# A two-dimensional transform and two feed-forward layers on one core: the lone rows' share computed once and added to the sums of a group

## The chip, the cores and the metric

The kernel runs on one core of a Trainium2 chip. A core has a matrix engine (TensorE; PE for its products, PEld for its weight loads), VectorE (DVE), ScalarE (ACT), GpSimd (POOL) and SyncE (SP), which here only issues DMAs; 16 DMA engines move data between HBM and the on-chip memory SBUF. Products are summed in PSUM. The metric is the time of one execution on the device, in microseconds, as the median of several runs.

## The reference

```python
def _attn_ref(x):                      # x: 8 x 3072 x 256
    X = np.fft.fft(x, axis=1)
    X = np.fft.fft(X, axis=2)
    return X.real.astype(np.float32)

def _moe_ref(x, w_in, w_out):          # w_in 256 x 2048, w_out 2048 x 256
    h = x @ w_in
    g = h - np.tanh(h)
    return (g @ w_out).astype(np.float32)

def _moe2_ref(x, w_in, w_out, g_ln):   # w_in 256 x 1024, w_out 1024 x 256
    h = x @ w_in
    e = np.exp(h - np.max(h, axis=-1, keepdims=True))
    sm = e / (np.sum(e, axis=-1, keepdims=True) + 1e-09)
    solu = h * sm
    mu = np.mean(solu, axis=-1, keepdims=True)
    var = np.mean((solu - mu) ** 2, axis=-1, keepdims=True)
    ln = (solu - mu) / np.sqrt(var + 1e-06) * g_ln
    return (ln @ w_out).astype(np.float32)
```

The transform's 8 x 3072 rows are the tokens of the first layer, whose output is the input of the second.

## The kernel before

The program has two parts that follow each other.

**The transform.** The 3072 rows of a batch are taken in sets of eight that the transform along the sequence treats alike; there are 384 such places, in three blocks (j = 0, 1, 2) of 128. With 8 batches that makes 24 iterations q = 3b + j. For each, SP loads a block `x` of 1 MB (`load_next("x")`, L296, three buffers). DVE adds and subtracts its parts (`prep`: `sm` L440, `cv` L445, `pm` L450, for j = 1 also L456), and PE multiplies the result with tables of cosines and sines (`transform`: `odd_class` L479, `even_classes` L498 and L507; tables `tts`, loaded by `table`, L352). The sums of a batch fill the eight PSUM banks, and after j = 2 `evict` copies them with ACT to `zt` and on to DRAM (`z1_d`, `z2_d`).

The first of the 384 places stands for no full set: its rows, 0, 384, 768 and so on of each batch, are the *lone rows*, eight per batch. They are loaded as `x8` (three copies of eight rows in partitions 0, 32 and 64, for a high and a low half). DVE and ACT turn them into `hl8` (`prep_8`: L416, L166, L169). For every batch PE adds their share to the sums, with four products against the small table `t8s`, whose columns repeat with a period of four (`lone_products`, L518).

The same loop prepares the weights. Twelve pieces are loaded in the order of `w_when`, narrowed from 64-bit words by two ACT steps (L201, L202) and three DVE steps (`narrow`: L205, L208, L211), and stored or, for the first four, multiplied with a table (`fold_w_in`, L389). `weave` interleaves such works with the preparation of iteration q + 2 step by step; the order of instructions on each engine is the program's order. The Nyquist column is loaded as `nraw` (L651) and `n8`, and prepared by `prep_nu` (L575 to L581), which is woven with `prep(3)`; `transform_nu` (L611) comes ahead of `transform(3)`.

**The loop.** 48 groups of 256 column pairs (six per batch), 16 steps each. In each step PE computes a block of the first layer (`ab`, L847), DVE adds the rank-one part and forms two halves (L858, L870, L871), ACT takes tanh (L877), DVE subtracts (L882), ACT rounds to a high half `gh` (L166), and POOL makes the low half (L169). `o1` (L901) multiplies high and low halves two steps later; its six products per step are in the order high, high, low. `layer2` spreads the second layer of the group before over the steps (products L934, L1039 and L1046; store by POOL at L1088 at every fourth step).

For the next group, `load_z` loads even and odd sums `zf` from DRAM at step 3. At step 7 `sum_z` adds and subtracts them for both halves u (L271, four POOL instructions of 128 columns), and at step 11 the results `zc` are split into high and low `zs`. For the first two groups this work is done on DVE, in the transform (iterations 15 and 18).

Issues of DMAs: SP's queue takes nearly all; ACT's takes the stores of `z2_d`. Eight semaphores count the landings of the DMAs of both.

Of the kernel before, what the change touches and what calls it, by code (L numbers as in the profile page):

```python
# [82 lines left out]
def tables():  # L83
# [18 lines left out]
    t24 = np.concatenate([c2, -c2, c4, s2, s4, -s4], 1)  # L102
# [6 lines left out]
    t8 = np.stack([np.cos(ang(k, r, 8)), np.sin(ang(k, r, 8)) * sign], 1).reshape(8, 2, 3, 4)  # L109
    t8h, t8l = split(t8)  # L110
    t8x = np.zeros((96, 2, 3, 4), np.float32)
# [28 lines left out]
def fft2_moe_moe_kernel(  # L140
# [11 lines left out]
    wo_d = dram.tile([4, P, 4, D], F32, name="wo_d")  # L152
    wi2_d = dram.tile([2, P, FF2], F32, name="wi2_d")
# [8 lines left out]
    z1536 = keep.tile([P, 3, B], F32, name="z1536")  # L162
    zh = keep.tile([P, 2, B], F32R, name="zh")
# [74 lines left out]
    t8s = tab.tile([96, 2, 3, 4], F32R, name="t8s")  # L238
    hl8 = tab.tile([96, B, 256], F32R, name="hl8")
# [89 lines left out]
    for q, w in zip((8, 11, 14, 16, 18, 20, 22, 23), w_rest):  # L329
# [18 lines left out]
    def table(j, k):  # L348

        edges = (0, 2 * NS, 2 * NS + TU, TT)  # L350
        o = slice(edges[k], edges[k + 1])
        nc.sync.dma_start(out=tts[:, j, o], in_=tt[j * P : (j + 1) * P, o])  # L352
# [4 lines left out]
    for i in range(8):  # L357
        pn = ps.tile([P, 512], F32, tag="ps", name=f"p_none{i}")
        for _ in range(3 if i < 6 else 2):
# [3 lines left out]
    for parts in ([(0, 0)], [(0, 1), (0, 2)], [(1, 0)]):  # L363
# [45 lines left out]
    def prep_8():  # L409
        r8 = raws.pop("x8").rearrange("p (b d) -> p b d", b=B)[0:96]  # L410
        parts = []
        for i in range(2):
            bs = slice(i * B // 2, (i + 1) * B // 2)
            eo8 = scratch(f"eo8_{i}").rearrange("p (b d) -> p b d", b=B // 2)[0:96]
            for u, op in ((0, ALU.add), (1, ALU.subtract)):
                nc.vector.tensor_tensor(  # L416
                    out=eo8[:, :, u * P : (u + 1) * P], in0=r8[:, bs, :P], in1=r8[:, bs, P:], op=op
                )
            rnd(hl8[:, bs], eo8)
            parts.append((bs, eo8))  # L420
            yield
# [870 lines left out]
```

## Time and profile before

| | |
|---|---|
| median of three runs | 2693.86 us (2693.49 to 2694.44) |
| the profiled execution: its time, its span | 2695.17 us, 2693.4 us |
| PE products, weight loads, busy | 2679.4 us, 2396.0 us |
| DVE, ACT, POOL busy | 2361.1 us, 1874.9 us, 2105.7 us |
| first product of the loop | 159.66 us after the span's start |
| mean granted PE clock | 0.999 of 2.4 GHz |

The span runs from the first to the last instruction that the profiler recorded. Busy time counts the instructions of an engine while they execute, not its waits and not the issue of DMAs. An average over the span hides that the transform and the loop have different limits, so times below are those of stretches.

### The profile page before, as it was taken

The page shows a single profiled execution, that of the slowest core. Times are in us where ns is not written, and L with a number is a line of the kernel's source. Part 1 is how long each engine was busy: PE and PEld are TensorE (multiplying, and loading weights), DVE is VectorE, ACT ScalarE, POOL GpSimd, SP SyncE. Part 2 cuts the span into 40 slices and gives each one's busy share as a digit, 9 for nine tenths or more (in the row PEclk, how much of TensorE's full clock was granted, in tenths as well). Part 3 has the DMA queues.
Part 4 walks back from the last instruction along what each step waited for, and adds up shares of the span by engine and source line. Part 5 has one row for each costly group of instructions (what it writes and reads, how often), then busy time and mean ns, then how long its engine had stood idle before and what let it go on. Part 6 is the DMA issues. An engine that isn't in the chain of part 4 may idle for free.

```text
span 2693.4 us, 47817 instructions
## 1 busy us (share of the span) xinstructions
PE 2679.4 (99%) x15348; PEld 2396.0 (89%) x15348; DVE 2361.1 (88%) x4789; ACT 1874.9 (70%) x3414; POOL 2105.7 (78%) x2786
## 2 busy tenths in 40 slices
PE   9999999999999999999999999999999999999999
PEld 5688999999999999999999999999999999999998
DVE  8988898888988888888988888888888889888886
ACT  3566777777777777777777777777777777767776
POOL 0057888888888888888888888888888888888885
PEclk9999999999999999999999999999999999999999
DMA  9953444444444444444444444444444444444442
GB/s 367 364 195 70 98 95 100 102 95 95 108 96 95 101 102 96 94 106 98 95 106 97 98 95 107 95 95 108 95 99 99 102 95 96 106 97 99 97 95 52
DMA packets 882842, 303.29 MB, mean 113 GB/s; under 512 B 788528, under 2 KB 844080, under 8 KB 879296
## 3 DMA queue, kind: packets, MB, share of 16 engines
q1 hardware_dynamic: 879984, 293.74, 44.0%
q10 hardware_dynamic: 2304, 6.42, 0.6%
q8 instruction: 123, 2.02, 0.3%
q14 instruction: 127, 1.04, 0.1%
q0 software_dynamic: 304, 0.07, 0.0%
HBM read 161.55 MB, written 138.60 MB: 111 GB/s over the span
## 4 chain that ended last, share of the span: by engine, by line
PE 92%; DVE 5%; DMA 1%; issue 1%; ACT 1%; POOL 0%; ACTq 0%; SPq 0%; DVEq 0%
PE x2p L901 36%; PE ab L847 19%; PE ph L934 18%; PE po L1039 12%; PE po L1046 6%; DVE cv L445 1%; DVE sm L440 1%; DVE pm L450 1%; DMA tts<-tt 0%; DMA wi_d<-wi_f 0%; DMA wo<-w_out 0%; DVE g L882 0%; DVE wi_f L211 0%; PE pt L1020 0%; POOL gh L169 0%
## 5 line engine op out<-in xcount | busy, mean ns | idle before, releaser
L901 PE MATMUL x2p<-gh,wo 128*128 128x512 f32 x4608 | 1122.5, 380 | 1.4 <-POOL gh L169 1.2
L169 POOL TENSOR_TENSOR gh<-g,gh 128x512 fp32r<-128x512 f32 x768 | 986.9, 1285 | 173.1 <-ACT gh L166 173.0
L901 PEld LDWEIGHTS x2p<-gh,wo 128*128 128x128 f32 x4608 | 826.6, 190 | 105.3 <-POOL gh L169 3.1
L877 ACT ACTIVATE t<-h 128x512 f32<-128x512 f32 x758 | 453.7, 599 | 462.7 <-DVE h L871 380.1
L847 PEld LDWEIGHTS ab<-zs,wt 128*128 128x128 f32 x4608 | 633.8, 191 | 43.6 <-ACT zt L566 2.3
L847 PE MATMUL ab<-zs,wt 128*128 128x256 f32 x4608 | 638.6, 275 | 1.9 <-ACT zt L566 1.6
L882 DVE TENSOR_TENSOR g<-h,t 128x512 f32<-128x512 f32 x758 | 514.4, 679 | 142.1 <-ACT t L877 120.6
L166 ACT ACTIVATE gh<-g 128x512 fp32r<-128x512 f32 x768 | 480.8, 626 | 153.4 <-DVE g L882 152.1
L934 PE MATMUL ph<-wi,x2s 128*128 128x512 f32 x2304 | 561.6, 380 | 1.1 <-POOL x2s L169 1.1
L169 POOL TENSOR_TENSOR ut<-um,ut 128x512 fp32r<-128x512 f32 x372 | 478.1, 1285 | 56.2 <-ACT ut L166 56.2
L1039 PE MATMUL po<-wo,ut 128*128 128x512 f32 x1528 | 521.4, 382 | 0.0
L934 PEld LDWEIGHTS ph<-wi,x2s 128*128 128x128 f32 x2304 | 421.7, 190 | 53.3 <-POOL x2s L169 1.5
L858 DVE SCALAR_TENSOR_TENSOR asb<-nb,wnu,ab 128x256 f32<-128x256 f32 x768 | 362.7, 472 | 85.4 <-PE ab L847 63.1
L1046 PE MATMUL po<-wo,ut 128*128 128x256 f32 x1528 | 416.5, 273 | 0.0
L870 DVE TENSOR_TENSOR h<-asb,ab 128x256 f32<-128x256 f32 x758 | 324.9, 429 | 26.1
L871 DVE TENSOR_TENSOR h<-asb,ab 128x256 f32<-128x256 f32 x758 | 324.6, 428 | 26.2
L1039 PEld LDWEIGHTS po<-wo,ut 128*128 128x128 f32 x1528 | 289.9, 190 | 30.3
L1046 PEld LDWEIGHTS po<-wo,ut 128*128 128x128 f32 x1528 | 293.4, 192 | 0.0
L949 ACT ACTIVATE e<-ph,st 128x1024 f32<-128x1024 f32 x192 | 214.9, 1119 | 96.7 <-PE x2p L901 60.3
L944 DVE TENSOR_REDUCE st<-ph 128x1 f32<-128x1024 f32 x192 | 233.6, 1217 | 4.5 <-PE ph L934 4.4
L958 DVE SCALAR_TENSOR_TENSOR u<-ph,e 128x1024 f32<-128x1024 f32 x192 | 233.6, 1217 | 3.5 <-ACT e L949 1.6
L166 ACT ACTIVATE ut<-um 128x512 fp32r<-128x512 f32 x372 | 233.5, 628 | 0.0
(123 smaller groups left out, 2229.7 us busy)
## 6 DMA issues: line engine op xcount, KB each, us to landing
mv_d<-tb SPq DMA_DIRECT2D x186, 512.0 KB, 2.6
um<-mv_d SPq DMA_DIRECT2D x744, 128.0 KB, 3.8
out<-o SPq DMA_DIRECT2D x192, 128.0 KB, 1.7
x<-xr SPq DMA_DIRECT2D x23, 1024.0 KB, 10.3
zf<-z_d SPq DMA_DIRECT2D x64, 128.0 KB, 2.7
z_d<-zt ACTq DMA_DIRECT2D x16, 392.0 KB, 7.3
wi<-w_in SPq DMA_DIRECT2D x6, 1024.0 KB, 9.2
z_d<-zt SPq DMA_DIRECT2D x16, 384.0 KB, 10.2
```

Of the source, the lines that this page charges most:

```text
L166: nc.scalar.activation(out=o, in_=i, func=AF.Copy)
L169: eng.tensor_tensor(out=o, in0=i, in1=hi.bitcast(F32), op=ALU.subtract)
L847: nc.tensor.matmul(in_pairs(pab[:, u]), wt[c][:, hw, u, o : o + P], in_turn(zs[:, hz, u]), start=(i == 0), stop=(i == 2),)
L858: nc.vector.scalar_tensor_tensor(out=asb, in0=zg[n][1], scalar=wnu[:, m : m + 1], in1=pab[:, 0], op0=ALU.mult, op1=ALU.add)
L870: nc.vector.tensor_tensor(out=h[:, 0], in0=asb, in1=pab[:, 1], op=ALU.add)
L871: nc.vector.tensor_tensor(out=h[:, 1], in0=asb, in1=pab[:, 1], op=ALU.subtract)
L877: nc.scalar.activation(out=t, in_=h, func=AF.Tanh)
L882: nc.vector.tensor_tensor(out=g, in0=hs.pop((n, m)).rearrange("p u n -> p (u n)"), in1=ts_.pop((n, m)).rearrange("p u n -> p (u n)"), op=A ...
L901: nc.tensor.matmul(in_pairs(x2p[n][mt]), wo1[c][:, hw, k, mt * P : (mt + 1) * P], in_turn(gh[:, hg]), start=(m == 0 and i == 0), stop=(m = ...
L934: nc.tensor.matmul(in_pairs(ph[:, fs]), xs[:, hx, k], in_turn(wi2[:, hw, k, fs]), start=(k == 0 and q == 0), stop=(k == 1 and q == 2),)
L1039: nc.tensor.matmul(in_pairs(po), ut[:, 0, ks], wo2[:, k].rearrange("p h x n -> p (x n) h"), start=(k == 0), stop=False,)
L1046: nc.tensor.matmul(in_pairs(po[:, :D]), ut[:, 1, ks], wo2[:, k, :, 0].rearrange("p h n -> p n h"), start=False, stop=(k == NK2 - 1),)
```

## The change

The lone rows' share of the transform has only 20 distinct columns for each batch and half u: four for each class, and four columns of two kinds again with the sign or the turn that the second window of a group needs. After the change PE computes these columns once (`lone_rows`, 16 products of 20 columns in iteration 3), ACT copies them to the tile `lone`, and `sum_z` adds them, repeated, to the sums of a group (`add_lone`): on POOL in the loop, on DVE for the first two groups. The four products per batch go. `lone` also goes into the special column `z1536`.

```diff
+    lone = keep.tile([P, B, 2, 5, 4], F32, name="lone")
...
+    def add_lone(n, u, eng, o):
+
+        b, g = divmod(n, GPB)
+        h, rows = g - NSJ, lone[:, b, u]
+        if h <= 0:
+            o = o.rearrange("p (a c) -> p a c", c=4)
+            add = rows[:, 1 if h == 0 else 0].unsqueeze(1).to_broadcast([P, GP // 4, 4])
+        else:
+            s = 4 if h == 1 else 2
+            o = o.rearrange("p (s a c) -> p s a c", s=s, c=4)
+            add = rows[:, 1:5] if h == 1 else rows[:, 2:5:2]
+            add = add.unsqueeze(2).to_broadcast([P, s, GP // 4 // s, 4])
+        return eng.tensor_tensor(out=o, in0=o, in1=add, op=ALU.add)
+
     def sum_z(n, u, eng):
...
+        return add_lone(n, u, eng, o)
...
-    def lone_products(u, lone, stop=False):
-        for pss, i, n in ((acc[1, u], slice(0, 1), NS), (acc[2, u], slice(1, 3), 2 * NB)):
...
+    def lone_rows():
+        pl = ps.tile([P, 512], F32, tag="ps", name="pl")[:, : B * 40].rearrange("p (b u k) -> p b u k", b=B, u=2)
+        for b in range(B):
+            for u in range(2):
+                nc.tensor.matmul(
+                    pl[:, b, u],
+                    hl8[u][:, b * P : (b + 1) * P].bitcast(F32R),
+                    t8s[:, u].rearrange("p c k -> p (c k)"),
+                    start=True,
+                    stop=True,
+                )
+        nc.scalar.copy(out=lone.rearrange("p b u c k -> p b u (c k)"), in_=pl)
...
         if q == 3:
             transform_nu()
+            lone_rows()
...
             for u in range(2):
-                if j == 7:
+                if j == 6 + u:
                     sum_z(n + 1, u, nc.gpsimd)
```

The beginning is rearranged. The lone rows are loaded once, as 64 rows, on ACT's queue; DVE and ACT split them, ACT stores the halves to DRAM and loads them back, in six DMAs, into the three places of two tiles that POOL has set to zero.

```diff
+    hl8 = [fold.tile([P, 1024], F32, tag="cw", bufs=4, name=f"hl8_{u}")[:96] for u in range(2)]
+    for h in hl8:
+        nc.gpsimd.memset(h, 0.0)
+    r8 = zp.tile([P, GP], F32, tag="nb", name="r8")[: 8 * B]
+    s8 = zp.tile([P, 2, 2, GP], F32R, tag="zs", name="s8")[: 8 * B, 0]
+    nc.scalar.dma_start(out=r8, in_=x8[0:8].rearrange("r b d -> (r b) d"))
...
     def prep_8():
...
+        eo8 = zp.tile([P, GP], F32, tag="zc", name="eo8")[: 8 * B]
+        for u, op in ((0, ALU.add), (1, ALU.subtract)):
+            nc.vector.tensor_tensor(out=eo8[:, u * P : (u + 1) * P], in0=r8[:, :P], in1=r8[:, P:], op=op)
+        rnd(s8[:, 0], eo8)
+        rest(nc.vector, s8[:, 1], eo8, s8[:, 0])
+        nc.scalar.dma_start(out=s8_d, in_=s8.bitcast(F32))
+        rows = s8_d.rearrange("(r b) w (u d) -> r w u b d", b=B, u=2)
+        for g, w in enumerate((0, 0, 1)):
+            for u in range(2):
+                to = hl8[u][32 * g : 32 * g + 8].rearrange("p (b d) -> p b d", b=B)
+                nc.scalar.dma_start(out=to, in_=rows[:, w, u])
```

The tables of the even classes come without their negatives (two thirds of the columns); ACT computes these for j = 0 and 2. The loads of tables and of x stand in another order, the products of zeros at the start are 27 in place of 22, in three banks in place of eight, and the last six pieces of the weights are loaded and narrowed one iteration earlier.

```diff
-    t24 = np.concatenate([c2, -c2, c4, s2, s4, -s4], 1)
+    t24 = np.concatenate([c2, c4, s2, s4], 1)
...
-    for q, w in zip((8, 11, 14, 16, 18, 20, 22, 23), w_rest):
+    for q, w in zip((8, 11, 13, 15, 17, 19, 21, 22), w_rest):
...
-        if q == 3 - 1:
-
-            coming["x"].append(("x8", lambda raw: [(raw[0:96], x8.rearrange("p b d -> p (b d)"))]))
...
+    def negatives(j):
+        for u, (at, of) in enumerate(((1, 0), (2, 1))):
+            nc.scalar.activation(out=triple(j, u)[:, at], in_=triple(j, u)[:, of], func=AF.Copy, scale=-1.0)
...
-    for parts in ([(0, 0)], [(0, 1), (0, 2)], [(1, 0)]):
+    for parts in ([(0, 0)], [(0, 1), (0, 2), (1, 0)], [(1, 1), (1, 2)]):
         load_next("x")
...
     now, folds = [], []
+    prep_8()
     weave(prep(0))
-    for j, k in ((1, 1), (1, 2), (2, 0), (2, 1), (2, 2)):
+    negatives(0)
+    for j, k in ((2, 0), (2, 1), (2, 2)):
         table(j, k)
...
     weave(prep(2))
+    negatives(2)
     load_next("w")
-    weave(prep_8())
     weave(prep(3), prep_nu())
```

## Rows read from the trace of the kernel before

**Rows 1.** The page, part 1: busy time, share of the span and instructions.
```profile
PE 2679.4 (99%) x15348; PEld 2396.0 (89%) x15348; DVE 2361.1 (88%) x4789; ACT 1874.9 (70%) x3414; POOL 2105.7 (78%) x2786
```

**Rows 2.** Windows: stretch, length, busy us of each engine, clock, DMA, GB/s.
```profile
10.00:20.00 10.00, 7.59 (x24) 3.98 (x22) 9.21 (x14) 0.00 (x0) 0.00 (x0) 1.00 1.03 346
...
100.00:125.00 25.00, 25.00 (x112) 17.11 (x112) 25.00 (x36) 12.99 (x22) 1.70 (x3) 1.00 1.01 366
...
1000.00:1052.00 52.00, 52.00 (x304) 47.33 (x303) 46.62 (x102) 37.40 (x69) 43.97 (x59) 1.00 0.43 100
```

**Rows 3.** Timeline, end of the transform: start, us, engine, line, operation, idle before.
```profile
150.14 1.29 DVE L450 TENSOR_TENSOR pm<-cv 128x512 f32<-128x512 f32 x2
...
151.55 0.96 PE L518 MATMUL pz<-t8s,hl 96*128 96x384 f32 x4
...
152.44 2.95 PE L479 MATMUL pz<-tts,pm 64*128 64x384 f32 x16
...
155.12 2.90 PE L498 MATMUL pz<-tts,pm 64*128 64x392 f32 x16
...
157.10 1.60 ACT L556 COPY zt<-pz 128x384 f32<-128x384 f32 x4
...
159.66 1.60 PE L847 MATMUL ab<-zs,wt 128*128 128x256 f32 x12 [1.63 <-ACT zt L566]
```

**Rows 4.** Timeline, beginning.
```profile
11.90 2.80 PE L498 MATMUL pz<-tts,pm 128*128 128x392 f32 x8
...
16.12 0.38 SPq L651 DMA_DIRECT2D nraw<-xn  x1
...
19.07 2.49 DVE L416 TENSOR_TENSOR eo<-x 96x512 f32<-96x512 f32 x4
...
25.75 1.23 DVE L440 TENSOR_TENSOR sm<-x 128x1024 f32<-128x1024 f32 x1 [1.81 <-DMA x<-xr]
...
26.90 0.18 DVE L575 TENSOR_TENSOR nraw<-nraw 128x32 f32<-128x32 f32 x1
```

**Rows 5.** Groups by line and shape, PE: busy us, mean ns | idle.
```profile
L822 PE MATMUL aside<-zh,wt 128*128 128x8 f32 x48 | 5.8, 245 | 0.0
```

**Rows 6.** Groups by line and shape, DVE.
```profile
L169 DVE TENSOR_TENSOR hl<-eo,hl 32x1024 fp32r<-32x1024 f32 x2 | 2.4, 1212 | 0.0
...
L169 DVE TENSOR_TENSOR zs<-zc,zs 128x256 fp32r<-128x256 f32 x4 | 1.5, 416 | 0.0
...
L205 DVE TENSOR_SCALAR wo_f<-wo_f 128x1024 f32<-128x1024 f32 x6 | 4.1, 688 | 1.6 <-ACT wo_f L201 1.6
...
L208 DVE SCALAR_TENSOR_TENSOR wo_f<-wo_f,wo 128x1024 uint32<-128x1024 uint32 x6 | 7.3, 1221 | 0.4 <-ACT wo L202 0.4
```

**Rows 7.** DMA issues up to 160 us: KB, median us to landing.
```profile
nraw<-xn SPq DMA_DIRECT2D x1, 96.0 KB, 9.9
```

**Rows 8.** Waits of SP's queue: us in total, times, longest.
```profile
SPq L296 <- DMA x<-xr: 13.3, 7, 3.0
```

**Rows 9.** The page, part 6: a short transfer on a nearly idle queue.
```profile
out<-o SPq DMA_DIRECT2D x192, 128.0 KB, 1.7
```

**Rows 10.** Groups by line and shape, POOL.
```profile
L1088 POOL TENSOR_TENSOR o<-o 128x256 f32<-128x256 f32 x191 | 140.9, 738 | 13.7 <-ACT o L1056 13.7
```

**Rows 11.** Timeline of the loop, POOL and PE, steps 6 to 9 of a group.
```profile
1002.52 1.29 POOL L169 TENSOR_TENSOR gh<-g,gh 128x512 fp32r<-128x512 f32 x1 [0.62 <-ACT gh L166]
...
1004.18 1.46 PE L901 MATMUL x2p<-gh,wo 128*128 128x512 f32 x6
...
1004.38 0.74 POOL L169 TENSOR_TENSOR x2s<-x2f,x2s 128x256 fp32r<-128x256 f32 x1 [0.57 <-PE ab L847]
...
1005.07 1.52 POOL L271 TENSOR_TENSOR zc<-zf 128x128 f32<-128x128 f32 x4
...
1010.65 1.29 POOL L169 TENSOR_TENSOR gh<-g,gh 128x512 fp32r<-128x512 f32 x1
...
1012.01 1.46 PE L901 MATMUL x2p<-gh,wo 128*128 128x512 f32 x6
```

More of the change, by code (lines that the diff above doesn't have):

```diff
@@ L237, in fft2_moe_moe_kernel @@
     tts = tab.tile([P, NSJ, TT], F32, name="tts")
[L238 to L239 removed]
+    t8s = tab.tile([96, 2, 5, 4], F32R, name="t8s")
+    hl8 = [fold.tile([P, 1024], F32, tag="cw", bufs=4, name=f"hl8_{u}")[:96] for u in range(2)]
[4 more added lines that the diff above has]
+    nc.scalar.dma_start(out=r8, in_=x8[0:8].rearrange("r b d -> (r b) d"))
     wnu = keep.tile([P, NM], F32, name="wnu")
@@ L348, in table, with triple @@
     def table(j, k):
-        edges = (0, 2 * NS, 2 * NS + TU, TT)
-        o = slice(edges[k], edges[k + 1])
-        nc.sync.dma_start(out=tts[:, j, o], in_=tt[j * P : (j + 1) * P, o])
+        if k == 0:
+            nc.sync.dma_start(out=tts[:, j, : 2 * NS], in_=tt[j * P : (j + 1) * P, : 2 * NS])
+            return
+        src = tt[j * P : (j + 1) * P, 2 * NS + (k - 1) * 2 * NB : 2 * NS + k * 2 * NB]
+        to = triple(j, k - 1)[:, 0 : 4 - k : 3 - k]
+        nc.sync.dma_start(out=to, in_=src.rearrange("p (t n) -> p t n", t=2))
+    def triple(j, u):
+        return tts[:, j, 2 * NS + u * TU : 2 * NS + (u + 1) * TU].rearrange("p (t n) -> p t n", t=3)
+    def negatives(j):
+        for u, (at, of) in enumerate(((1, 0), (2, 1))):
+            nc.scalar.activation(out=triple(j, u)[:, at], in_=triple(j, u)[:, of], func=AF.Copy, scale=-1.0)
     nothing = wt[3][:, 0, 0]
     nc.vector.memset(nothing.bitcast(F32), 0.0)
-    for i in range(8):
+    for i in range(3):
         pn = ps.tile([P, 512], F32, tag="ps", name=f"p_none{i}")
-        for _ in range(3 if i < 6 else 2):
+        for _ in range(9):
             nc.tensor.matmul(pn, nothing[:, :P], nothing, start=True, stop=True)
-    for parts in ([(0, 0)], [(0, 1), (0, 2)], [(1, 0)]):
+    for parts in ([(0, 0)], [(0, 1), (0, 2), (1, 0)], [(1, 1), (1, 2)]):
         load_next("x")
@@ L409, in prep_8 @@
     def prep_8():
[L410 to L421, printed above, removed]
-        load_next("x")
-        for bs, eo8 in parts:
-            yield rest(nc.vector, hl8[64:96, bs], eo8[64:96], hl8[64:96, bs])
+        eo8 = zp.tile([P, GP], F32, tag="zc", name="eo8")[: 8 * B]
[9 more added lines that the diff above has]
+                nc.scalar.dma_start(out=to, in_=rows[:, w, u])
     FOLDED = 1
@@ L483, in odd_class, with even_classes @@
                     start=(half == 0 and j == w),
-                    stop=(j == 2 and half == 1 and not (last_lone and w == 0)),
+                    stop=(j == 2 and half == 1),
                 )
-    def even_classes(q, u, pss, last_lone):
+    def even_classes(q, u, pss):
         j = q % NSJ
@@ L502, in even_classes @@
                         start=(half == 0 and j == w),
-                        stop=(j == 2 and half == 1 and not (last_lone and w == 0)),
+                        stop=(j == 2 and half == 1),
                     )
@@ L534, in transform @@
         b, j = divmod(q, NSJ)
-        def lone():
-            for u in range(2):
-                lone_products(u, hl8[:, b, u * P : (u + 1) * P], stop=(b == 0))
-        if j == 2 and b:
-            lone()
         for cls, products in ((1, odd_class), (2, even_classes)):
@@ L545, in transform @@
                     acc[cls, u] = sums(f"pz{b}_{cls}_{u}")
-                products(q, u, acc[cls, u], b == 0)
-        if j == 2 and not b:
-            lone()
+                products(q, u, acc[cls, u])
         hl.pop(q)
@@ L563, in evict @@
                 if b == B - 1:
-                    nc.gpsimd.tensor_tensor(out=z1536[:, 2], in0=z1536[:, 0], in1=z1536[:, 1], op=ALU.subtract)
+                    z = z1536[:, 2]
+                    nc.gpsimd.tensor_tensor(out=z, in0=z1536[:, 0], in1=z1536[:, 1], op=ALU.subtract)
+                    nc.gpsimd.tensor_tensor(out=z, in0=z, in1=lone[:, :, 0, 2, 0], op=ALU.add)
             for w, p in enumerate(acc.pop((2, u))):
```

14 lines of the change are left out of this document (4 added, 10 removed).

## The prediction

> **What bounds the kernel now.** I read the page first. The matrix engine (PE) is busy 99% of the span, VectorE (DVE) 88%, GpSimd (POOL) 78% [rows 1]: a change can matter only where it shortens what PE waits for, or makes it wait. The span has two parts, and I asked for the windows of each. In the loop (1000 to 1052 us, one group of 16 steps) PE is busy for all of the 52 us, POOL for 43.97, DVE for 46.62: PE sets the pace there, and nothing of this change takes PE work out of the loop. In the transform, which lasts until the loop's first product at 159.66, PE *and* DVE are full at once: both 25.00 of 25.00 us from 100 to 125 [rows 2].
>
> Which of the two sets the transform's end decides this case, and the timeline of its end answers it. DVE prepares the rows of iteration q two iterations ahead of PE. It finishes the last preparation (pm, q = 23) at 150.14 + 1.29 = 151.43; PE starts that iteration at 152.44, after the lone products of 151.55 [rows 3]. So at the end PE is only 1.0 us behind DVE. DVE itself has, from 26.90 on, nothing to wait for; the window from 100 to 125 shows it without a hole [rows 2]. Its work from 26.90 to 151.43 is a rigid block of 124.5 us, and whoever shortens PE by more than 1.0 us finds DVE as the bound. The block begins at 26.90 with nraw (the Nyquist column), behind x3, whose sums ran from 25.75 after 1.81 us of waiting for a DMA [rows 4].
>
> **The change part by part.**
>
> *Lone products out of PE.* Four matmuls per batch, from 151.55 to the next instruction at 152.44, 0.9 us [rows 3]: 8 x 0.9 = 7.2 us of PE go. In come 16 matmuls of 20 columns, each with 128 weight columns. Nearest row: the 48 matmuls of 8 columns at L822, 5.8 us, 0.12 each [rows 5]: +1.9 us once, in iteration 3. Net -5.3 us for PE; but only 1.0 us of it can be seen unless DVE's block moves too.
>
> *Lone rows out of DVE's beginning.* Four sums of 96x512, 2.49 us from 19.07 [rows 4], and two lows of 32x1024, 2.4 us [rows 6], become two 64x128 sums and one 64x256 low ahead of the first preparation. A 128x256 step takes 0.42 [rows 6], so the new ones cost under 1.3 us, and what hides them is that DVE later waits for nraw in any case; without that wait they would shift the block by that much. For the same reason the 4.9 us that go do not come off the start of the block: it starts when nraw has landed. The load of nraw stays behind the load that prep(1) issues. That was x3 and becomes x4, because x8 no longer takes a place in the queue. Bytes ahead of nraw: less 0.79 MB (x8) and 0.60 MB (a third of six tables), plus 1.05 MB (x4), plus 0.39 MB on ACT's queue (r8, s8 out to DRAM, six loads of 32 KB). At the 346 GB/s of the window from 10 to 20 [rows 2] the first three make -1.0 us, the ACT transfers +1.1. (The Trainium skill, "DMA: Bandwidth & Descriptors", section "Issuing engines are not separate DMA queues", has DMAs of all issuing engines interleave on the same 16 DMA engines. By that rule the +1.1 stands; a queue of its own would make it 0.) nraw was issued at 16.12 and took 9.9 us [rows 4, 7]: it landed at 26.0 and lands near 26.1. DVE would take it at once, 0.8 earlier than 26.90.
>
> Against that stands a limit on the DMAs under way. Seven issues at the line that loads x waited 13.3 us in all for another load of x to land, up to 3.0 at a time [rows 8]; by the order of issues that other one is the eighth before. r8 and the seven DMAs of prep_8 now stand in this row ahead of x3, so x3 may be issued only when a table (1,1) or (1,2) is in and SP's queue has run dry. I price the hole at up to 1.7 us, what a short transfer on an idle queue takes from issue to landing [rows 9]. So the block starts between 1.9 us earlier (ACT's bytes cost nothing, no hole) and 0.9 later. I take 0.0, the hole being nearly certain and its size not.
>
> *Added to DVE's block.* The first two groups' sums get four adds of 128x256 on DVE: 0.416 each [rows 6], less the overlap of some 0.04 that such rows show in a chain: +1.5 us (bounds: 1.1, and 3.0 if the repeated operand doubled them). The weights of iteration 22 move to 21, the one that prep(23) is woven into: two of their three DVE steps, 0.688 and 1.221 [rows 6], less 0.08 overlap each, now come before the last pm: +1.75. They ran after it so far.
>
> *End of the transform.* PE's last product ends at 155.12 + 2.90 = 158.02. ACT began to empty the sums at 157.10, because it narrowed the last weights first, and the loop's first product waited until 159.66 for it [rows 3]. With the weights one iteration earlier four copies of 0.4 run beside the last products; what remains after them is the copies of the even sums. I take 0.4 us off, bounds 0 and 0.8.
>
> *Negatives, copies.* Four ACT steps of 128x196 and one copy of 128x320, each under the 0.4 of a copy of 384 columns [rows 3]. ACT does nothing from 10 to 20 us [rows 2], which hides the first two if ACT isn't held by its own DMA issues (a rival below).
>
> *The loop.* 46 groups get two adds of 128x256 on POOL. Nearest row: 0.738, contiguous [rows 10]; the sums of 128 columns beside them read two runs of 64 and take 1.52 for four [rows 11], no more per column. I take 0.74 for each. They lie in POOL's gaps. Sums and add of u = 0 now come at step 6, ahead of the gh of 1002.52: 0.76 + 0.74 = 1.50 into a gap of 0.62, so that gh ends 0.88 later, at 1004.69. PE needs it for the fifth of the six matmuls from 1004.18, which start (1.46 - 0.38)/5 = 0.216 apart: at 1005.04, 0.35 to spare. The gap of 0.57 before x2s leaves 0.31 of lateness; step 7 does 1.50 in place of 1.52. The gh from 1010.65 ends at 1011.94 and is needed at 1012.01 + 0.86: 0.93 to spare against 0.3 [rows 11]. Cost: nothing; at most 2 us where groups have less slack.
>
> *Sum.* Last pm: 151.43 + 0.0 + 1.5 + 1.75 = 154.7. PE starts q = 23 there in place of 152.44: +2.25. Less 0.4 at the end: +1.85 us; loop 0. The profiled execution took 2695.17 us with a span of 2693.4; the median of the runs is 2693.86, 1.3 lower, and the shift goes onto the median: **2695.7 us**. The ends of the terms make -0.9 (-1.9, 1.1, 0.8 off) and +6.6 (+0.9, 3.0, no gain at the end, 2 in the loop; the 1.75 in both, the 1.0 of PE's lag off); ends do not come together, and 2693 to 2699 holds nearly all of this case.
>
> **The rivals.**
>
> *DVE gives way and PE's gain is seen (faster).* If PE stayed the bound, the end would move by -5.3 and -0.4: 2688.2 us. For it: DVE does lose 4.9 us of work, and x3 comes early. Against it: the last pm would have to be done at about 147, so the block, 3.25 longer, would have to start at 19, before x4 and nraw can be in. Chance 0.10, part gains included.
>
> *POOL's adds are dear (slower).* At a price c for an add the lateness is 0.76 + c - 0.62 - 0.57 after x2s and 2c - 1.19 after step 7; PE stalls once that passes 0.93, so from c = 1.06 us. At twice the contiguous row, 1.48, the stall is 0.84 us in each of 46 groups: +39 us, 2734. For it: no row has an operand repeated in runs of four columns. Against it: runs of 64 cost nothing extra [rows 11]. Chance 0.10. The Trainium skill, "GPSIMD Engine Reference", section 7, speaks for this rival: many small read commands cost about 102 cycles each, without overlap. By that rule, were each of the 64 repeats a command of its own, one add would take some 5 us (an estimate from that page); no row here shows such an operand.
>
> *The beginning holds PE up (slower).* ACT issues the loads of hl8 itself, each behind s8's way to DRAM and one of the eight, and the negatives stand behind them in ACT's order. PE's even products of q = 0, at 11.90 so far [rows 4], wait for the negatives, perhaps until 18. That alone is hidden: PE would be ready for q = 23 at 152.44 - 7 x 0.9 + 1.9 + 6.1 = 154.1, just before DVE's 154.7. If the granted clock fell to its lower level in that hole and some 8 us of products took twice as long, PE would be 7 us behind DVE: 2703 us. Against it: the clock is 1.00 from 10 to 20 us, where PE is busy only 7.59 of 10 [rows 2]. Chance 0.06.
>
> **How the numbers follow.** DVE as the bound, no difference that counts: 0.74. The rivals: 0.10, 0.10, 0.06. A difference of 0.2%, 5.4 us, is about what a measurement of this kernel can tell from none. The likeliest case lies inside it but for 0.02 on the slow side: faster 0.10, same 0.72, slower 0.18. The range reaches from 2691 (part gains of the first rival) to 2701 (lesser forms of the two others).
>
> **What would show it.** Right: no lone products in L518's place; DVE without a hole from about 27 to 155; PE with small waits on pm in the last iterations, where it had none; the loop's first product between 160 and 163; POOL's new adds near 0.74, and PE still 52.0 of 52 us per group. Wrong: that first product before 158 or after 165; an add over 1.06 us; x2p products that wait for gh; a granted clock under 1 before 40 us.

## The result, and the profile after

The changed kernel takes 2712.59 us (median of 6 runs, 2710.39 to 2714.84), the kernel before on the same chip 2694.51: a ratio of 1.0066, 95% interval 1.0053 to 1.0079. It is slower by 18 us. Predicted were 2695.7 us and a range of 2691 to 2701. The profiled execution took 2713.05 us with a span of 2711.2, against 2693.4 before.

Windows first, the stretches of [rows 2] and of the loop's start, of the changed kernel:

```profile
10.00:20.00 10.00, 3.53 (x11) 1.82 (x10) 8.58 (x14) 0.36 (x2) 0.00 (x0) 0.99 0.63 234
20.00:32.00 12.00, 11.40 (x45) 7.90 (x47) 3.36 (x5) 0.99 (x4) 0.00 (x0) 0.87 1.03 378
42.00:50.00 8.00, 8.00 (x26) 4.84 (x26) 7.86 (x12) 1.42 (x4) 0.00 (x0) 0.79 1.03 427
100.00:125.00 25.00, 18.57 (x68) 11.28 (x67) 20.08 (x29) 10.39 (x19) 1.43 (x2) 0.87 0.85 299
172.00:225.00 53.00, 50.68 (x296) 45.38 (x295) 42.38 (x88) 34.50 (x63) 37.07 (x30) 0.97 0.29 99
225.00:278.00 53.00, 49.45 (x276) 43.84 (x275) 42.51 (x88) 34.03 (x62) 39.50 (x51) 0.94 0.30 69
1000.00:1052.00 52.00, 52.00 (x305) 47.33 (x304) 47.17 (x107) 37.10 (x69) 44.68 (x61) 1.00 0.43 98
```

The loop's group is untouched: PE still 52.00 of 52, POOL 44.68 in place of 43.97. All 17.8 us of span are lost ahead of 278 us, in three places: the beginning (the DMAs move 234 GB/s from 10 to 20, before 346), the middle (DVE 20.08 of 25 from 100 to 125, before 25.00) and the loop's first groups.

The end of the transform divides them; timeline of it, changed kernel:

```profile
163.48 1.28 DVE L478 TENSOR_TENSOR pm<-cv 128x512 f32<-128x512 f32 x2
...
165.60 2.96 PE L507 MATMUL pz<-tts,pm 64*128 64x384 f32 x16
...
171.12 1.16 PE L874 MATMUL ab<-zs,wt 128*128 128x256 f32 x8
```

The loop's first product moved from 159.66 [rows 3] to 171.12, by 11.5 us; the other 6.3 are lost between there and 278 us. DVE's last pm is done at 164.76 (before 151.43), and the lone products are gone from the place ahead of 165.60.

**The beginning.** Timeline, changed kernel:

```profile
12.76 6.83 ACTq L452 DMA_DIRECT2D hl<-s_d  x6
...
18.63 0.89 SPq L376 DMA_DIRECT2D tts<-tt  x2
19.64 0.62 ACT L383 ACTIVATE tts<-tts 128x196 f32<-128x196 f32 x2 [15.71 <-DMA hl<-s_d]
19.65 0.34 SPq L320 DMA_DIRECT2D x<-xr  x1
...
20.06 3.76 PE L526 MATMUL pz<-tts,pm 128*128 128x392 f32 x6 [4.71 <-ACT tts L383]
...
32.08 0.19 DVE L599 TENSOR_TENSOR nraw<-nraw 128x32 f32<-128x32 f32 x1 [3.70 <-DMA nraw<-xn]
```

and the waits of SP's queue up to 32 us:

```profile
SPq L376 <- DMA hl<-s_d: 7.8, 1, 7.8
```

Read the two queues side by side. ACT issues the six loads of hl8 (L452) from 12.76 to 19.59, because they wait for s8 to be in DRAM and for turns among the transfers under way; the negatives (L383) come behind them, at 19.64. SP's next two table loads wait 7.8 us for the first of those same loads, so x3 is issued at 19.65 and nraw at 23.35 (before 16.12 [rows 4]). nraw is in at 32.08: DVE's block starts 5.2 us later. PE's even products of q = 0, at 11.90 before [rows 4], run at 20.06, six of them in 3.76 us where eight took 2.80: the lower of the clock's two levels, 1.2 GHz, behind a wait of 4.71.

**The middle.** Timeline, changed kernel:

```profile
118.29 1.13 ACT L205 ACTIVATE wo_f<-wo 128x1024 f32<-128x1024 f32 x1 [9.14 <-DMA wo<-w_out]
120.35 1.60 ACT L578 COPY zt<-pz 128x384 f32<-128x384 f32 x4
...
120.86 4.63 PE L420 MATMUL pw<-wi_f,ftab 128*128 128x512 f32 x5 [6.12 <-ACT zt L578]
```

ACT has come to narrow w_out before it is loaded. It waits 9.14 us; behind it in ACT's order stand the copies that empty the sums, behind those PE, and DVE has only 20.08 us of work in 25. The load itself was issued late, 5.6 us before ACT got it, because SP first waited 9.3 us for DVE's last narrowing step of an earlier piece, whose buffer the load takes:

```profile
SPq L320 <- DVE wi_f L215: 9.3, 1, 9.3
...
112.66 0.38 SPq L320 DMA_DIRECT2D wo<-w_out  x1
```

**The loop's start.** Timeline, ACT's second gh and then a stretch of step 6 of the loop's second group, changed kernel:

```profile
181.06 0.63 ACT L170 ACTIVATE gh<-g 128x512 fp32r<-128x512 f32 x1 [3.70 <-DMA z_d<-zt]
...
232.64 0.78 POOL L280 TENSOR_TENSOR zc<-zf 128x128 f32<-128x128 f32 x2
233.50 0.61 POOL L294 TENSOR_TENSOR zc<-zc,lone 128x256 f32<-128x256 f32 x1
234.06 1.27 POOL L173 TENSOR_TENSOR gh<-g,gh 128x512 fp32r<-128x512 f32 x1
...
235.38 1.22 PE L928 MATMUL x2p<-gh,wo 128*128 128x512 f32 x2 [2.38 <-DVE asb L885]
```

and the same place of the kernel before:

```profile
217.67 1.27 POOL L169 TENSOR_TENSOR gh<-g,gh 128x512 fp32r<-128x512 f32 x1
...
219.00 0.75 PE L901 MATMUL x2p<-gh,wo 128*128 128x512 f32 x2 [0.96 <-POOL gh L169]
```

The first line is a wait for storage: the tile gh may be written only when the store of zt has left the place where gh now lies. In the others, POOL's sums and add for u = 0 (1.4 us) have slipped in ahead of gh, in a group in which POOL also splits w_out2. That gh ends at 235.33, and PE, which starts at 235.38, has waited 2.38 us in place of 0.96 (the row names DVE's `asb`, which ended at 235.37; in the kernel before PE went on ahead of that step). The two windows from 172 to 278 us of the kernel before:

```profile
172.00:225.00 53.00, 51.64 (x289) 45.46 (x289) 43.52 (x89) 35.83 (x66) 41.61 (x42) 0.97 0.14 47
225.00:278.00 53.00, 51.93 (x305) 46.87 (x304) 47.02 (x94) 37.94 (x70) 42.45 (x54) 1.00 0.41 91
```

Both traces can be laid side by side by the products of `o1`, 96 in each group. From the loop's first product to the first of `o1` both kernels take 6.75 us. From there to `o1` of the next group it is 37.83 us in place of 34.31, to that of the third 55.97 in place of 53.23, and 52.28 in both kernels from then on. So the loss at the loop's start is 3.5 us in the first group and 2.7 in the second, waits and clock together, and nothing later.

### The profile page after: what moved, and what is told of

The parts are those of the page before. It is cut to its first block, busy times and chain, and to the rows that moved or that the text cites. A ratio compares the mean times of both kernels' runs of the same rounds, so it can differ in the third digit from the quotient of the medians.

```text
span 2711.2 us, 47892 instructions
## 1 busy us (share of the span) xinstructions
PE 2685.9 (99%) x15337; PEld 2399.0 (88%) x15337; DVE 2359.9 (87%) x4790; ACT 1876.6 (69%) x3418; POOL 2161.7 (80%) x2881
## 4 chain that ended last, share of the span: by engine, by line
PE 96%; DMA 2%; DVE 1%; ACT 0%; issue 0%; POOL 0%; SPq 0%; ACTq 0%; POOLq 0%; DVEq 0%
PE x2p L928 36%; PE ab L874 19%; PE ph L961 18%; PE po L1066 12%; PE po L1073 6%; PE pz L507 2%; PE pz L526 1%; DMA wo<-w_out 1%; PE pw L420 0%; DMA z_d<-zt 0%; DMA nraw<-xn 0%; DMA tts<-tt 0%; PE pz L535 0%; DMA x<-xr 0%; PE pt L1047 0%
```

## The experiments

Kernels whose names begin with a, c, d and f1, f3, f6 are edits of the changed kernel, the others edits of the kernel before. The ratio behind each time is to runs of the kernel before on the same chip; intervals are about +-0.1%, so that differences under 2 us between two experiments are not told apart. The kernel before took 2694.5 to 2696.1 us on the chips of this study. What an edit brings is therefore counted from the kernel before on its own chip: the changed kernel is 18.1 us above it. Times inside an execution come from one profile of each kernel.

### The two named places, undone one at a time

**a1_weights_back**

```
-    for q, w in zip((8, 11, 13, 15, 17, 19, 21, 22), w_rest):
+    for q, w in zip((8, 11, 14, 16, 18, 20, 22, 23), w_rest):
```

> The changed kernel with the iterations in which the weights are narrowed as they were (8, 11, 14, 16, 18, 20, 22, 23). Theory (the 18 us have two sources, the beginning about 5 and the earlier weights about 6, the rest following from them at the loop's start): ACT's waits for w_out fall from 9.1 us to under 1 near 115 to 125 us, DVE is full there, the loop's first product moves from 171.4 to about 164 to 166, and the run takes 2703 to 2707. Rival 1 (the beginning alone costs the time): no change, 2712. Rival 2 (the weights alone): 2694 to 2697.

2707.84 us, 1.0045 (1.003 to 1.006): 12.7 above the kernel before, 5.4 us off, about the theory's least. DVE is full again from 100 to 125 (24.93 of 25) and the first product comes at 164.24, 6.9 us earlier; but from there to the first product of `o1` it takes 11.90 us in place of 6.75, at a clock of 0.94 from 150 to 172 and 0.93 from 172 to 225, and ACT's gh waits 5.36 us for the store of zt.

**a2_reload_late** (the six loads in a function of their own)

```
     negatives(2)
+    reload_8()
```

> The changed kernel with the six loads of hl8 issued after the second pair of negatives, where nothing of the beginning stands behind them. Theory (ACT's and SP's orders are held by those loads): the negatives run at about 11 to 12 us, PE's even products of q = 0 right behind them, nraw is in at about 27 in place of 32, the clock is 1.00 until 40 us, the loop's first product comes about 5 us earlier, and the run takes 2705 to 2708. Rival (the bytes ahead of nraw or x3's place in the queue cost the time, not the loads' place): nraw still at 31 or later, 2711 to 2713.

2708.27 us, 1.0049 (1.0034 to 1.0064), 5.0 off. The negatives run at 13.45 and nraw is in at 26.01, as foreseen, but of six microseconds 1.3 arrive at the loop's first product (the rest of the gain lies in the first two groups): at their new place the loads hold ACT again, and DVE's block, which waits for ACT behind them, is 137.2 us long in place of 132.7. ACT's timeline:

```profile
23.28 8.93 ACTq L454 DMA_DIRECT2D hl<-s_d  x6
32.26 0.21 ACT L170 ACTIVATE n8hl<-n 96x8 fp32r<-96x8 f32 x1 [8.70 <-DMA hl<-s_d]
32.38 1.59 ACT L580 COPY zt<-pz 128x384 f32<-128x384 f32 x4
```

**a3_reload_pool**

```
-                nc.scalar.dma_start(out=to, in_=rows[:, w, u])
+                nc.gpsimd.dma_start(out=to, in_=rows[:, w, u])
```

> The changed kernel with the six loads of hl8 issued by POOL, at the same place of the program. If ACT's order is what costs: as with the late reload, negatives at about 12 us and 2705 to 2708. If it is SP's queue, in which table loads wait for the turn of those loads: the negatives are early, but x3 is issued near 19 us as in the changed kernel and nraw is in at 31 to 32, 2709 to 2712. If the loads no longer stand in SP's row of eight either, nraw is in at about 27.

2706.02 us, 1.0040 (1.0025 to 1.0055), 7.2 off. POOL waits where ACT did, and nothing that is needed soon stands behind it; the negatives run at 11.80, x3 is issued at 13.4, nraw is in at 28.25. So ACT's order and SP's wait were the cost; what the bytes cost lies inside the spread of kernels that begin as before the change (26.9 to 29.3, below).

**a4_both**: a1 and a2 together.

> The changed kernel with the late reload and the old iterations of the weights. Theory (the two sources add, and the loss at the loop's start follows from the shift of the weights and the late transform): first product of the loop at 158 to 161, 2693 to 2697, the same as before the change. Rival (the loop's start has a cause of its own, +6 us): first product as said, but 2699 to 2703.

2703.98 us, 1.0030 (1.0017 to 1.0043), 9.2 off, where 5.4 and 5.0 would make 10.4. The first product is at 161.39, but the first of `o1` 12.88 us behind it. The rival holds: the loop's start has causes of its own.

**b1_weights**

```
-    for q, w in zip((8, 11, 14, 16, 18, 20, 22, 23), w_rest):
+    for q, w in zip((8, 11, 13, 15, 17, 19, 21, 22), w_rest):
```

> The kernel before with only the iterations of the weights changed (8, 11, 13, 15, 17, 19, 21, 22). Theory (weights one iteration earlier are asked for before they can be in, whatever the beginning does): ACT waits 4 to 9 us for w_out near 100 to 125, DVE is no longer full there, the loop's first product comes at 164 to 168, and the run takes 2699 to 2703. Rival (the late beginning makes them late; on time they cost only DVE's 1.75 us, as predicted): first product at 160 to 161.5, 2695 to 2697.

2703.12 us, 1.0027 (1.0017 to 1.0037), 7.4 slower with a beginning that is as it was. From 100 to 125, and ACT's wait in it:

```profile
100.00:125.00 25.00, 19.39 (x68) 12.23 (x67) 20.65 (x31) 11.69 (x20) 1.91 (x3) 0.86 0.83 292
...
115.49 1.13 ACT L201 ACTIVATE wo_f<-wo 128x1024 f32<-128x1024 f32 x1 [9.04 <-DMA wo<-w_out]
```

The earlier weights alone make the wait of the changed kernel (9.04 and 9.14). DVE's block is 130.7 us here (29.33 to 160.06) in place of 124.5: 6.2 more.

Why the piece is late can be read from the same trace. There are two buffers for pieces, and the load of the next one is issued when a narrowing is over. The new list puts a second piece into iteration 13, which already had one, and the DVE steps of the two are woven. The second piece is not in yet: ACT waits 5.25 us for it, until 102.23. So the last step of the first piece comes at 108.67 (before 102.18), and the next load, for which SP stands 9.0 us, at 109.99 (before 103.50). The loads of zf, behind it in SP's order, cost DVE another 2.0 us. The DMAs meanwhile have nothing to do, with a share of 0.03 and 14 GB/s:

```profile
108.67 1.22 DVE L211 SCALAR_TENSOR_TENSOR wi_f<-wi,wi_f 128x1024 uint32<-128x1024 uint32 x1
...
109.99 0.38 SPq L296 DMA_DIRECT2D wo<-w_out  x1
...
107.00:110.00 3.00, 3.00 (x13) 2.12 (x13) 3.00 (x5) 0.00 (x0) 0.00 (x0) 0.66 0.03 14
```

No run moves the later pieces without this meeting in iteration 13, so what an earlier narrowing would cost without it is not known.

### The loop's start

**c1_pad**

```
+    spare_tab = tab.tile([P, 1696], F32, name="spare_tab")
```

> The changed kernel with 6.8 KB per partition of unused storage set aside among the transform's tables, so that the second tile gh of the loop no longer lies where the last odd sums (zt) wait to be stored. Theory (the smaller hl8 moved the tiles of the transform against those of the loop, and ACT's gh at 181.06 waits 3.7 us for that store): ACT's wait for z_d<-zt at the loop's start is gone, PE's wait of 1.7 us there and the drop of the clock behind it too, and 1.5 to 4 us come off: 2708 to 2711. Rival (gh waits for a load, or for the late end of the transform, and the address is by the way): the wait stays or turns up in another tile, 2712 to 2713.

2708.53 us, 1.0047 (1.0034 to 1.0060), 5.3 off with not one instruction changed; in the trace the first group takes 34.34 us again, 3.5 less. hl8 no longer lies among the tables, so all behind them moved down by 8 KB; in the built program of the changed kernel the second gh lies at bytes 90112 to 94208 of each partition and the last odd sums at 91648 to 94784. With the pad they are at 98432; the wait for the store is gone and the window reads

```profile
172.00:225.00 53.00, 52.31 (x312) 46.72 (x313) 44.65 (x94) 36.32 (x66) 39.95 (x32) 1.00 0.28 97
```

**c2_at7**

```
-                if j == 6 + u:
+                if j == 7:
```

> The changed kernel with POOL's sums for u = 0 back at step 7, behind those for u = 1. Theory (in the first group with sums on POOL the split of w_out2 takes the slack, and the sums ahead of gh hold PE for 2.4 us at 235.38, after which the clock falls for some 7 us): PE's wait there goes back to about 1.0, as before the change, and 3 to 5 us come off: 2708 to 2710. Rival (step 6 costs nothing, as predicted, and that wait has another cause): 2712 to 2713. A third: four adds and sums in one step, 4 x 0.62 + 1.5 us, hold PE in later groups: over 2715.

2726.41 us, 1.0113 (1.0100 to 1.0127). The theory holds in the second group (PE's wait is 0.96 us again), and the third guess holds in all later ones: four sums and two adds in one step hold PE in every group (51.70 of 52 us busy from 1000 to 1052), and a group takes 52.66 us in place of 52.28, 0.38 more. The new step is right for the loop and wrong for its first group on POOL.

**a5_add_twice** (its output counts the lone rows twice)

```
+        add_lone(n, u, eng, o)
         return add_lone(n, u, eng, o)
```

> The changed kernel with every add of the lone rows on POOL done twice (its output counts those rows twice). The slack that the prediction worked out: an add of c = 0.62 us leaves PE's gh in time, and PE waits once c passes 1.06 us; at 2 x 0.62 = 1.23 us the lateness of 2c - 1.19 = 1.27 passes 0.93 by 0.34 us in each of 46 groups: 14 to 18 us more, 2726 to 2731. Rival (the gaps lie where they do no harm, or POOL catches up elsewhere): under 2716.

2727.29 us, 1.0118 (1.0105 to 1.0132), 13.1 more than the changed kernel, each counted from the kernel before on its chip. In the trace a group takes 52.62 us in place of 52.28: 0.34 more, which is what the prediction's sum of gaps gives.

### The lone rows alone

**b2_core** and **b4_core_step**: the kernel before with `lone_rows`, `add_lone` and the five-column table, loads and order as they were. b4 has in addition

```
-                if j == 6 + u:
+                if j == (7 if n == 1 else 6 + u):
```

> The kernel before with the lone rows computed once and added to the sums, and nothing else: x8 is loaded and split as before, tables and weights as before (hl8 lies in two of the buffers for the folded weights, since the tables leave no room for it beside the new tile). Theory: the beginning and the middle are as before, PE loses its eight lone products, the loop's first product is at 159 to 161.5; the loop's start still loses the wait of gh for the store and the one at step 6, 4 to 8 us in all: 2699 to 2702. Rival (all of the 18 us lie in the beginning and the weights): 2692 to 2696.

> The kernel before with the lone rows computed once, as in b2_core, and in addition the sums of the first group that POOL adds (group 2, in the loop's second group of steps) at step 7 again. Theory (in b2_core 2.4 us of PE's wait in that group and the clock behind it come from the sums ahead of gh): PE's wait there is about 1.0, 2 to 4 us come off 2704.3: 2700 to 2702. Rival (that wait follows from the transform's end): 2703 to 2705.

2704.30 us, 1.0030 (1.0019 to 1.0040), and 2701.56, 1.0020 (1.0011 to 1.0029). DVE's block is 126.4 us in both (b2: 29.09 to 155.53): the four adds cost 1.9. The core alone is slower than no change, 8.6 us in b2 and 5.5 in b4, whose second group takes 52.09 us where b2's takes 55.95. And in b2's windows the clock is low at the transform's end, with a beginning and weights that are those of before:

```profile
150.00:172.00 22.00, 17.41 (x102) 14.52 (x100) 18.23 (x31) 11.45 (x22) 3.80 (x7) 0.91 0.84 267
```

**b5_core_pool** (b4 with POOL for the lone rows' sums and lows and the first groups' adds)

```
-            yield rest(nc.vector, hl8[i][64:96], eo8[64:96], hl8[i][64:96])
+            yield rest(nc.gpsimd, hl8[i][64:96], eo8[64:96], hl8[i][64:96])
...
-        return add_lone(n, u, eng, o)
+        return add_lone(n, u, nc.gpsimd, o)
```

> b4_core_step with POOL, idle in the transform, in place of DVE for the sums and lows of the lone rows and for the four adds of the first two groups. Theory (DVE's block sets the transform's end, and its start waits for x3 and nraw): the block is 124.5 us again and starts at 26 to 27, the loop's first product comes at 156 to 160, and the run takes 2693 to 2698. Rival 1 (POOL's share of the storage port slows DVE beside it): DVE's steps beside POOL's are longer, no gain. Rival 2 (PE, freed, waits for DVE and loses its clock at the end): clock under 0.95 from 150 to 172, 2698 to 2702.

2704.93 us, 1.0036 (1.0024 to 1.0049): the theory failed. DVE waited 8.6 us for POOL's lows: the six steps take POOL 9.59 us from 20 to 32, where DVE takes 4.9 [rows 4, 6], so its block began at 32.

**d1_mended**: the edits of a2, a1 and c1, and the step of b4.

> The changed kernel with all four mended: late reload, old iterations of the weights, 6.8 KB set aside, and the sums for group 2 at step 7. Theory (the losses add: 4.3, 4.8, 4.1 and some 3 us off 2712.6): 2695 to 2699, the wait for z_d<-zt gone and PE's wait in the second group about 1.0. Rival (the clock's falls overlap, so that mends do not add): 2700 to 2704.

2701.80 us, 1.0022 (1.0013 to 1.0031). 12.3 of the 18.1 are back; the first product comes at 159.90, level with before. But from there to the first product of `o1` it takes 12.60 us in place of 6.75, nearly all that its span has over that of before (6.3), and the clock is low:

```profile
150.00:172.00 22.00, 19.96 (x101) 16.73 (x100) 17.42 (x30) 10.71 (x22) 4.24 (x7) 0.81 0.86 277
```

### What is left: PE with less to do

**f5_no_lone** and **g2_lone_last**: the kernel before with lone products left out and nothing in their place; those outputs lack the lone rows.

```
-        if j == 2 and b:
-            lone()
```

(in g2: `if j == 2 and b == B - 1:`)

> The kernel before with the lone products of batches 1 to 7 left out and nothing put in their place (so those outputs lack the lone rows): PE has 28 matmuls, 6.3 us, less to do, and no other engine has more. Prediction's reading (DVE's block sets the end, only the 1.0 us by which PE lags can be seen): 2692.5 to 2695. If PE were the bound: 2688 to 2690. Theory of the clock (PE with less to do waits for DVE at the end, and the clock falls over the loop's start): clock under 0.95 from 150 to 172 and 2697 to 2701, slower than with the products.

> f5_no_lone with the lone products of the last batch kept (those of batches 1 to 6 left out): 0.9 us more of PE, at the transform's end. If it is the end alone where the clock is lost: 2695 to 2697, with a clock of 1.00 from 150 to 172 in all runs. If PE's lead over DVE, built up over all batches, is what lets it wait and lose the clock: 2698 to 2702, as f5_no_lone.

2701.35 us, 1.0021 (1.0013 to 1.0030), and 2700.52, 1.0016 (1.0006 to 1.0025). Taking 6.3 us of products away from PE, and adding nothing anywhere, makes the kernel *slower*. The single runs go by the clock: four of g2's 12 have a mean granted clock of 0.999 and took 2695.7 to 2696.5 us, eight have 0.996 or 0.997 and took 2699.7 to 2705.9. f5's split in the same way (four at 0.999: 2696.8 to 2698.6; seven below: 2700.5 to 2705.2). Of the 97 runs of the kernel before beside all these experiments, two have 0.997, and they took 2701.1 and 2703.7. So the clock goes with the time in one and the same kernel, and its loss, rare before, is what most runs have once products are left out.

Where it is lost in those runs is not shown, since both profiles are of runs at 0.999. In f5's, PE waits 1.43 us for DVE's last pm and 3.19 for ACT, is busy 16.50 of the 22 us from 150 to 172, and the clock stays at 1.00; in g2's it is 0.92 there, and that run took 2695.69. b2's 0.91 and d1's 0.81 make the same place likely, no more. Nor is it told apart which products matter: those of the last batch alone did not keep the clock.

**f1_zero_products**, **f3_pool_mended**, **f6_pool_zero**: d1 with products of zeros in the lone products' place; d1 with POOL's reload in place of the late one; both.

```
+        if j == 2 and b:
+            for u in range(2):
+                for pss, n in ((acc[1, u], NS), (acc[2, u], 2 * NB)):
+                    nc.tensor.matmul(pss[0][:, :n], zeros[:96, :P], zeros[:96, :n], start=False, stop=False)
```

> d1_mended with four products of a tile of zeros in each batch after the first, where the kernel before has its lone products and of the same shapes (0.9 us of PE per batch, nothing added to the sums). Theory (what is left in d1_mended, 5.7 us, is the clock's fall at the loop's start, and it falls because PE, without the lone products, has less to do at the transform's end): the windows from 150 to 225 us show a clock of 0.95 to 1.00 in place of 0.81 and 0.98, and the run takes 2696 to 2698 although PE does 6 us more. Rival (PE's wait for ACT at the end, after the last narrowed weights, lowers the clock whatever PE does before): 2701 to 2703.

> d1_mended with the loads of hl8 on POOL at their place in the changed kernel, in place of the late ones on ACT. Theory (POOL waits for the store of s8 without holding anything, where ACT's late loads held its copies for some 9 us from 23 to 32): ACT has no wait for hl8 left, the block starts at 25 to 28, and 0 to 3 us come off d1_mended's 2701.8. Rival (the late loads cost nothing): the same as d1_mended within 1 us.

> f3_pool_mended with the zero products of f1_zero_products. If both theories hold: the clock near 1.00 from 150 to 225 and 2694 to 2697, level with the kernel before. If the zero products only cost PE time: 1 to 6 us over f3_pool_mended.

2700.57 us, 1.0017 (1.0008 to 1.0026); 2702.80, 1.0027 (1.0015 to 1.0039); 2700.99, 1.0018 (1.0010 to 1.0026). f1's windows from 150 and 172 us:

```profile
150.00:172.00 22.00, 21.57 (x124) 17.03 (x124) 18.28 (x31) 11.41 (x21) 2.63 (x7) 1.00 0.88 280
172.00:225.00 53.00, 51.64 (x300) 45.56 (x299) 43.66 (x92) 36.68 (x67) 42.49 (x37) 1.00 0.17 55
```

The clock is back, by work that computes nothing: all 11 runs of f1 have a mean of 0.998 or 0.999, where d1's have 0.996 or 0.997, and the first of `o1` follows the first product by 6.76 us again. The time is not back, within what can be told (5.2 above the kernel before, d1 5.7): PE, 6 us fuller, now ends the transform itself (q = 23 starts at 158.46, its pm was done at 155.65), and the first product comes at 163.97. f6 shows the same, with its first product at 167.86. f3 gained nothing over d1; its block starts at 30.78 and not at 25 to 28.

**g1_core_zero**: b4 with the zero products.

> b4_core_step (the beginning and the weights as before, the lone rows computed once) with four products of zeros in each batch after the first, in the place of the lone products. Theory (b4_core_step is at +5.5 because PE with less to do loses its clock at the transform's end; with the clock back only DVE's four adds, 1.5 us, are left): clock 0.97 to 1.00 from 150 to 225, 2696 to 2698. Rival (the time is lost elsewhere, in the beginning above all): 2700 to 2702.

2701.58 us, 1.0019 (1.0011 to 1.0028): the theory failed. Nine of its 11 runs have a mean clock of 0.998 or 0.999 and are no faster than b4's. Its profile is of one of the two others: DVE's block starts at 30.37, 3.5 us later than before, and the clock is 0.92 from 150 to 172 although the zero products are there.

The parts of one profile of each kernel, in us; from the third group on a group takes 52.28 in all of them:

| | DVE's block: start, length | last pm to first product | to the first of `o1` | first, second group |
|---|---|---|---|---|
| before | 26.90, 124.5 | 8.22 | 6.75 | 34.31, 53.23 |
| changed | 32.08, 132.7 | 6.35 | 6.75 | 37.83, 55.97 |
| b2 | 29.09, 126.4 | 6.85 | 9.55 | 35.35, 55.95 |
| b4 | 30.97, 126.4 | 7.80 | 11.47 | 35.29, 52.09 |
| d1 | 25.11, 129.8 | 4.97 | 12.60 | 34.54, 53.20 |
| f1 | 25.83, 129.8 | 8.32 | 6.76 | 34.32, 52.09 |
| f5 | 29.16, 124.6 | 8.23 | 7.23 | 34.27, 53.16 |
| g1 | 30.37, 126.4 | 6.83 | 9.02 | 35.44, 53.27 |

The column to the first of `o1` is where the lost clock is paid: 2.8 to 5.9 us in b2, b4 and d1. It does not show in the changed kernel, where PE is busy for all 22 us from 150 to 172; undoing the earlier weights brings it out (11.90 us in a1, 12.88 in a4).

## Why the prediction was wrong, point by point

- **What bounds the transform: right.** DVE's block as a rigid one held: 124.6 us in f5 with 28 of the 32 lone products gone, 126.4 with the adds, 130.7 with the earlier weights. The changed kernel's 132.7 (32.08 to 164.76) is 124.5 + 1.9 + 6.2. It is rigid only while nothing holds it from outside: with the reload late on ACT, DVE waits for ACT (in d1 1.9 us for n8hl and 1.4 for a weight) and the block is 129.8. PE's 7.2 us of lone products bought nothing.
- **"So the block starts between 1.9 us earlier [...] and 0.9 later [...]. I take 0.0": failed, +5.2.** The text named both causes and mis-sized them. (Five kernels with the new beginning start at 31.0 to 32.2, four with that of before at 26.9 to 29.3, so that the loss is 2 to 5 us, and 5.2 that of the two profiles compared.) The hole that it priced at up to 1.7 us, by one short transfer, was 7.8: the transfer SP waits for was itself queued behind s8's way to DRAM (its store issued at 4.42, the first load let go at 12.76 and in at 18.6). ACT's further loads wait their turn in the same way. A transfer of one engine was late, and the row of eight carried it into another engine's queue.
- **"+1.75" for the weights of iteration 22: failed, +6.2, the largest term.** The edit moves six of the eight, and only the last one's DVE steps were priced. The prediction did not ask whether a weight *is there* an iteration earlier. A load of w_out took 8.4 us from issue to narrowing in b1 (93.84 to 102.23), and ACT came 5.25 us too early for it; the next load could not be issued until that delay had worked through DVE, which made the 9.04. The queue of loads behind a buffer was late, and not the DMAs, whose share was 0.83 over that stretch of b1 and 1.01 before [rows 2]. The 4.4 us that DVE idles from 100 to 125 in b1, and 1.75, are the 6.2.
- **DVE's adds: right** (1.9 for 1.5). **The transform's end: right in size** (from last pm to first product 6.4 us in place of 8.2, so -1.9 for -1.4), but not shown to be so for the reasons given: without lone products alone it is 8.2 (f5), with the earlier weights alone 9.6 (b1), and d1, with the weights where they were, has 5.0. That may be luck. **lone_rows: right** (16 products, 1.95 us for 1.9). These terms give 5.2 + 1.9 + 6.2 - 1.9 = 11.4 of the 11.5 measured.
- **The loop at nothing: right from the third group on (52.28 us in both kernels), wrong for its start, +6.3.** The add took 0.616 us for the 0.74 taken; the slack worked out from rows was confirmed by a5 (0.34 us per group, as worked out). The Trainium skill, "GPSIMD Engine Reference", section 7, by which one add could take some 5 us (the prediction's estimate from that page), is not borne out here: 0.616 is less than the contiguous 0.738 of [rows 10]. The start lost to two things that were not looked for: a store whose place a later tile takes (c1: 3.5 us of the first group), and a group whose slack was smaller than that of the group read at 1000 us (the second: 52.85 in c2, 52.09 in b4, for 55.97). The prediction's "at most 2 us where groups have less slack" allowed for the second of them, too little, and for the first not at all.
- **The rival of the beginning** (0.06) described what happened, negatives behind the loads, even products held (20.06 where it said about 18), the clock falling (0.87 from 20 to 32). It then put it down as hidden but for the clock. PE's part *was* hidden by DVE; what was not is that DVE's own loads stood in the same queue.
- **"Only 1.0 us of it can be seen" was too kind to PE's gain.** f5 and g2 show the sign turned: their runs at a mean clock of 0.999 are no faster than before, and most of their runs lose clock that the loop, where PE is the bound, then needs. The rows first: clock 0.81 from 150 to 172 in d1, 1.00 with zero products in f1. The Trainium skill, "TensorE: Matmul & The Clock Gate", section "HAM oscillation — how this bites in real kernels", has the clock gate re-throttle PE across its waits for data; by that rule, d1's trace agrees, while f5's, with 4.6 us of waits in that window, kept 1.00.

**What stays open.** d1 leaves 5.7 us. In its trace they are the clock at the loop's first products, while DVE's longer block is made up for at the start and the end of the transform. f1 keeps that clock, but its first product comes 4.3 us later than before. g1 still loses 5.9; in its trace 3.5 us are the start of the block, 1.9 the adds, 3.4 the loop's first products and first group, and 1.4 come off at the transform's end. Whether the core delays the start is not settled: b4's block started at 30.97 and b2's at 29.09, but b1 and f5, whose first loads are those of before, start at 29.33 and 29.16, g2 at 27.82, before at 26.90. Kernels that begin alike differ by over 2 us, with one profile of each. And why the clock falls in most runs of f5 and g2, and in few of before, is not shown.

No kernel of the study beat the one before.

## What to carry to other kernels

Work that is brought forward must be asked two things: what it costs, and whether its data is there by then. Where a load is issued only when an earlier step gives its buffer back, bringing a step forward does not bring its load forward; it moves the wait to the head of an engine that works in program order, with everything behind it, and that delays the next load too. A small round trip through DRAM costs what is queued behind its issuing engine and behind its turn among the transfers, not its bytes. And an engine that is freed but not the bound gains nothing; if it is PE, look at the granted clock of the stage that follows.

## What the runs showed of the hardware that was not expected

- A tensor operation on POOL with an operand repeated in runs of four columns (128x256) took 0.616 us, the contiguous one 0.737: the repeat is not dear.
- With products on zeros in place of the lone products the granted clock was 1.00 from 150 to 225 us in f1's profile (d1 without them: 0.81 and 0.98); in g1's it fell all the same (0.92 and 0.97).
- Leaving out 28 of PE's 15,000 products (24 in g2) made two sets of runs of one kernel: 2696 to 2699 us at a mean clock of 0.999, 2700 to 2706 at 0.996 or 0.997.
- The free placement of tiles is a term of the time: 8 KB less storage among the tables cost 3.5 us of the first group until 6.8 KB were set aside unused.
